# One-word transfers in place of additions as gates of weight reads, two more gates, two sums moved, and another place for one operand

## The chip, the cores and the metric

The kernel runs on one core of a Trainium2 chip. The metric is the device time of one execution in microseconds (us), the median of several runs. TensorE (PE) does the matmuls, VectorE (DVE) and ScalarE (ACT) the elementwise work, GpSimd (POOL) some sums, and SyncE (SP) and POOL issue the transfers, each on a queue of its own. The kernel before takes 1507.99 us (three runs, 1507.09 to 1509.15).

## What is computed

A linear attention, whose output x has 4608 tokens of 512 values, goes through two feed-forward layers. Both have the same form, with weights of their own (512 x 2048 and back); in short:

```python
x = softmax(q, axis=-1) @ (softmax(k, axis=2).T @ v)   # per batch and head
for w_in, w_out in ((moe_w_in, moe_w_out), (moe2_w_in, moe2_w_out)):
    h = np.maximum(x @ w_in, 0.0)
    x = (h * h) @ w_out
```

Everything is float32.

## The kernel before, in words

**Sweeps and blocks.** The four products with weights are four sweeps f = 0 to 3 (`w_in` and `w_out` of the first layer, then of the second), each over 9 blocks j of 512 tokens. A float32 product is made of three matmuls on operands that were split into a high and a low part (`passes`, L444). In sweep 0 the blocks 0 to 5 are plain (`h`). All else is Strassen's scheme: 2 x 2 blocks and seven products instead of eight, so every operand is a tile of seven slices, high and low: two are blocks of the matrix itself (512 of its 1792 columns), five are sums or differences (1280).

**Names.** `n` are the products of sweep 0 from the token operand `v`, `y` those of sweeps 1 and 3 from the hidden operand `G` and the weight operand `W`, `m` those of sweep 2 from `x` and `W`. Names in full are `Wf_a` for operand a (0 to 7) of sweep f, `Gl_j_a` for layer l and block j, `xj_kk`; the page leaves the numbers out. In sweeps 1 and 3 a block takes its 8 operands in turn, seven products on each (`second_mm`, L506), and only at the end are its results made. In sweep 2 (and blocks 6 to 8 of sweep 0) a block has four units u of 84 matmuls (`first_mm`, L457); unit u uses the weight operands 2u and 2u+1. Where one sweep ends and the next begins the work of both is interleaved; the second sweep's first products come before the first one's last ones. These places are called first crossing (sweep 0 to 1), second (1 to 2) and third (2 to 3).

**How an operand is made.** A 512 KB load brings a matrix into SBUF. DVE makes the sums (`comb_add`, L96), ACT the high part (`comb_hi`, L108), DVE the low part (`comb_lo`, L121). A hidden operand is squared by ACT first, in place, in the tile that was loaded (`g_square`, L441; tiles `qc`, `qd`, `qe` by turns). `comb_hi` also sets where an operand lies in its tile: G, x and v have an offset of 8 words (PLAIN), 4 (EARLY) for G0_0_0 and all of x0, and others in layer 1. Of `v` the first high slice alone lies 4 words ahead of its place; `low` holds that view, and `first_mm` takes it for the product that reads this slice.

**Weights.** Weight operands in KEPT (L45) were made once and stored whole. They come as one read of 1792 KB by `get_operand` (L190), on POOL's queue. The others come as 512 KB (`get_w`, L175; tiles `qx`, `qa`) on SP's queue and are combined by DVE and ACT. Operand a goes to slot (a + 5) % 8 of eight, so that a read needs the slot's former operand to be done with. Four reads have a gate as well, by the table `behind` (L804): `touch` (L186), an addition of one word on POOL that reads from a loaded tile, goes ahead of the read in POOL's order. For W2_2 and W2_3 that tile is G0_8_7's.

**Order.** Every step is recorded with an engine, a model cost and a due time. A list scheduler (L604) runs the model and writes out each engine's order: on each engine, of the steps that could start the one with the earliest due time. The engines run their queues in this order and wait on semaphores.

**After the products.** `copy` (L475) takes two products out of PSUM, `both` (L478) adds them on POOL (on DVE for the first Strassen block), `rest` (L481) subtracts, `summed` (L487) and `plus` (L517) make results, `plus2` (L520) on POOL finishes those of sweep 1.

Of the kernel before, what the change touches and what calls it, by code (L numbers as in the profile page):

```python
# [21 lines left out]
P = 128  # L22
# [26 lines left out]
def linear_attention_two_relu2_ffn(ctx: ExitStack, tc: tile.TileContext, q0, k0, eye, qh, kh, vh, wio, out):  # L49
# [58 lines left out]
    def comb_hi(key, q, x, tag):  # L108
        if key not in hls:
            if key[0] in "Gxv":  # L110
                t = pool.tile([P, 14 * HB + SHIFT], F32R, name=key, tag=tag)
                o = LATE + 4 * (key in ("G1_0_0", "G1_0_1", "G1_2_0")) if key[:2] == "G1" else EARLY if key == "G0_0_0" or key[:2] == "x0" else PLAIN
                hls[key] = t[:, o:o + 14 * HB].rearrange("p (a b n) -> p a b n", a=2, b=7)
                if key[0] == "v":
                    low[key] = t[:, o - 4:o - 4 + 2 * (HB + 4)].rearrange("p (a n) -> p a n", a=2)[:, :, :HB]
            else:
                hls[key] = pool.tile([P, 2, 7, HB], F32R, name=key, tag=tag)
        r, src = (slice(0, 2), q[:, 0:4:3]) if x == 0 else (slice(2, 7), cfs[key])
        nc.scalar.activation(out=low[key] if x == 0 and key in low else hls[key][:, 0, r], in_=src, func=AF.Copy)  # L119
# [63 lines left out]
    def put_operand(f, a):  # L183
        nc.sync.dma_start(out=ready_w[f, a], in_=f32(hls.pop(f"S{f}_{a}")))

    def touch(f, a, key):  # L186
        one = pool.tile([P, 1], F32, name=f"touch{f}_{a}", tag="kvm")
        nc.gpsimd.tensor_tensor(out=one, in0=gq[key][:, 0, 0:1], in1=gq[key][:, 0, 0:1], op=ALU.add)  # L188

    def get_operand(f, a, tag):  # L190
        hls[f"W{f}_{a}"] = pool.tile([P, 2, 7, HB], F32R, name=f"W{f}_{a}", tag=tag)
# [265 lines left out]
    def first_mm(l, j, u, i, place):  # L457

        k, o = (l, j, u), BANK[i]
        if i == o:  # L460
            m[k, o] = bank(place, f"{'nm'[l]}{i}_{j}_{u}")
        for s in range(2):
            w = hls[f"W{2 * l}_{2 * u + s}"]
            terms = []
            for kk in range(2):
                x, c = hls[f"{'vx'[l]}{j}_{kk}"], slice(kk * P, (kk + 1) * P)
                high = x[:, 0, RIGHT[i]] if l or RIGHT[i] else low[f"v{j}_{kk}"][:, 0]
                terms.append((w[:, 0, LEFT[i], c], w[:, 1, LEFT[i], c], high, x[:, 1, RIGHT[i]]))
            passes(m[k, o][:, s], terms, start=i == o and s == 0)

# [330 lines left out]
    def slot_of(a):  # L801
        return f"w{(a + 5) % 8}"

    g_loads, g_place, behind = {}, {}, {(2, 2): (0, NB - 1, 7), (2, 3): (0, NB - 1, 7), (3, 5): (1, 0, 4), (3, 7): (1, 0, 6)}  # L804

    def weights(f, a, due):

        if (f, a) in KEPT:
            place = Place(slot_of(a))
            b = behind.get((f, a))  # L810
            if b:
                assert b in g_loads, (f, a)
            seen = op("POOL", 200, due - 9000, lambda: touch(f, a, b), [g_loads[b]], [g_place[b]]) if b else None
            l = op("POOL", 1400, due - 9000, lambda: get_operand(f, a, slot_of(a)), [*kept[f, a], seen, begun.get((f, a))], [place], lands=1792, port=False)
            combined[f"W{f}_{a}"] = [l], place
            return
        beside = Place(slot_of(a + 1)) if f == 0 and a not in (2, 7) else None
        place, new = quad_place("quad", 0, beside) if beside else quad_place(("qx", "qa")[a % 2] if f else "qc")
        after = [dma(due - 12000, lambda: get_w(f, a, new), 512, stashed[f, a], [place])]
        if beside:  # L820
            cf = Place("five", parent=beside), lambda: beside.area(4 * HB, 5 * HB).rearrange("p (a n) -> p a n", n=HB)
        else:
            cf = cf_place(("cf", ("att1", "att2")[a % 2], "att1", "att1")[f])
        combine(f"W{f}_{a}", slot_of(a), due, ("DVE",) * 3, lambda: wfs[f, a], place, after, *cf)
# [175 lines left out]
    def first(l, j, u):  # L1000
# [28 lines left out]
        c2 = copy_of(2, d + g)  # L1029
        mm(5, d + g, [M[2]])  # L1030
        c5 = copy_of(5, d + 2 * g)
        if (l, j) == (0, FIRST):
            s = op("DVE", dve(512), d + 3 * g, lambda: both(k, "DVE"), [c2, c5], [tt["s5"], tt["s2"]], port=True)
        else:
            s = op("POOL", gps(512), d + 3 * g, lambda: both(k), [c2, c5], [tt["s5"], tt["s2"]])
# [20 lines left out]
    def second(l, j, a):  # L1056
# [35 lines left out]
        for q, i, o, po in ((0, 7, 2, p21), (3, 6, 1, p12)):  # L1092
            tt[q] = t_place[k, q] = Place("t")
            if quick:
                y = op("DVE", dve(512), e + 2900, lambda q=q, o=o: plus3(k, q, o), [r, po], [tt[q], tt[o], tt["e"]], port=True)
                y = op("DVE", dve(512), e + 3000, lambda q=q, i=i: plus4(k, q, i), [y, M[i]], [tt[q], bk[i]])
            else:
                y = op("DVE", dve(512), e + 3000, lambda q=q, i=i: summed(k, q, i), [r, M[i]], [tt[q], bk[i], tt["s5"]])
                y = op("POOL", gps(512), e + 3600, lambda q=q, o=o: plus2(k, q, o), [y, po], [tt[q], tt[o]])
            y_stored[k, q] = dma(e + 5000, lambda q=q: put_y(k, q), 256, [y], [tt[q]])  # L1100

    spare = {}
# [139 lines left out]
```

## Time and profile before

| | |
|---|---|
| median of 3 runs | 1507.99 us |
| profiled execution | 1511.11 us |
| its span | 1509.3 us |
| busy PE / DVE / ACT / POOL | 1487.6 / 1190.4 / 971.0 / 253.6 us |
| DMA, mean over the span | 216 GB/s |

The rows come from the profiled execution alone; it lasted 3.1 us longer than the median of the runs, 1.8 us of it lie outside the span. Times of rows are microseconds from the span's start. `W<-o` is a read of a kept weight operand, `qx<-w` a 512 KB load, `[2.05 <-DVE t L488]` says that the engine stood idle for 2.05 us until DVE's `t` of line 488 was there.

### The profile page before, as it was taken

What the parts mean: (1) busy time and instruction counts of PE and PEld (TensorE: products, weight loads), DVE (VectorE), ACT (ScalarE), POOL (GpSimd) and SP (SyncE); (2) the same over time, 40 slices, a digit from 0 to 9 for tenths busy, and PEclk for the clock granted to TensorE, in tenths of its full rate; (3) what the DMA queues carried; (4) which work ended last, traced back from release to release, by engine and by line L of the source; (5) the groups of instructions that cost most, each with busy time, mean ns of one, the idle gap of its engine ahead of it and who ended that gap; (6) DMA issues with size and microseconds to landing.
All of it is one profiled execution on the core that took longest, in us unless ns stands there. A gap on an engine that the chain in (4) does not pass through costs nothing.

```text
span 1509.3 us, 30549 instructions
## 1 busy us (share of the span) xinstructions
PE 1487.6 (99%) x12036; PEld 1414.4 (94%) x12036; DVE 1190.4 (79%) x1823; ACT 971.0 (64%) x1617; POOL 253.6 (17%) x193
## 2 busy tenths in 40 slices
PE   6999999999999999999999999999999999999998
PEld 5788888789999999999999999999999999999998
DVE  7998777899867999999986455444456999999996
ACT  8987767787765666666654788787777443444442
POOL 1001000000110111111113153243311111111110
PEclk9999999999999999999999999999999999999999
DMA  9888989986759444444447677677669644444441
GB/s 368 287 292 319 342 319 336 346 295 204 228 189 328 167 146 138 140 139 140 140 139 273 222 233 257 206 259 249 197 202 325 207 146 136 138 137 138 138 137 55
DMA packets 154144, 326.63 MB, mean 216 GB/s; under 512 B 13072, under 2 KB 84880, under 8 KB 151184
## 3 DMA queue, kind: packets, MB, share of 16 engines
q1 hardware_dynamic: 152128, 300.83, 59.5%
q0 software_dynamic: 1872, 23.86, 4.4%
q8 instruction: 94, 1.54, 0.4%
q14 instruction: 50, 0.41, 0.1%
HBM read 189.63 MB, written 135.00 MB: 215 GB/s over the span
## 4 chain that ended last, share of the span: by engine, by line
PE 90%; DMA 3%; ACT 3%; DVE 2%; issue 1%; POOL 1%; SPq 0%; DVEq 0%; ACTq 0%; POOLq 0%
PE y L448 44%; PE m L448 22%; PE h L448 15%; PE n L448 5%; PE xps L405 2%; PE kvps L334 1%; DMA qx<-w 1%; DMA W<-o 1%; POOL touch L188 0%; ACT w L153 0%; ACT wf L162 0%; DMA w<-w 0%; DMA w<-wio 0%; DMA qc<-w 0%; DMA att<-vh 0%
## 5 line engine op out<-in xcount | busy, mean ns | idle before, releaser
L448 PE MATMUL y<-G,W 128*128 128x256 f32 x3024 | 345.3, 277 | 2.0 <-DVE t L488 2.0
L448 PE MATMUL m<-x,W 128*128 128x256 f32 x3024 | 345.7, 277 | 1.5 <-DMA W<-o 1.5
L448 PEld LDWEIGHTS y<-G,W 128*128 128x128 f32 x3024 | 344.8, 188 | 2.2 <-DVE t L488 2.2
L448 PEld LDWEIGHTS m<-x,W 128*128 128x128 f32 x3024 | 345.1, 188 | 1.7 <-DMA W<-o 1.7
L448 PE MATMUL y<-W,G 128*128 128x256 f32 x3024 | 343.9, 276 | 0.0
L448 PEld LDWEIGHTS y<-W,G 128*128 128x128 f32 x3024 | 343.7, 188 | 0.0
L448 PE MATMUL h<-hl,w 128*128 128x512 f32 x1080 | 259.9, 396 | 3.4 <-DVE w L84 3.4
L448 PEld LDWEIGHTS h<-hl,w 128*128 128x128 f32 x1080 | 200.4, 188 | 49.6 <-DVE w L84 5.7
L479 POOL TENSOR_TENSOR ts<-ts,ts 128x512 f32<-128x512 f32 x61 | 93.5, 1533 | 750.2 <-DVE t L518 460.4
L119 ACT ACTIVATE G<-hl 128x1280 fp32r<-128x1280 f32 (+1 forms) x95 | 86.4, 926 | 115.9 <-PE y L448 65.5
L488 DVE TENSOR_TENSOR t<-m,ts 128x512 f32<-128x512 f32 x72 | 49.1, 688 | 97.5 <-PE m L448 77.9
L125 DVE TENSOR_TENSOR G<-hl,G 128x512 fp32r<-128x512 f32 (+1 forms) x95 | 108.7, 1149 | 16.2 <-ACT G L119 15.2
L448 PE MATMUL n<-v,W 128*128 128x256 f32 x1008 | 120.3, 280 | 0.0
L448 PEld LDWEIGHTS n<-v,W 128*128 128x128 f32 x1008 | 117.1, 188 | 2.1 <-issue 1.7
L491 ACT ACTIVATE t<-t 128x512 f32<-128x512 f32 x96 | 59.8, 628 | 56.2 <-DVE t L488 51.8
L494 ACT ACTIVATE t<-t 128x512 f32<-128x512 f32 x144 | 88.5, 627 | 2.3
L125 DVE TENSOR_TENSOR G<-cf,G 128x1280 fp32r<-128x1280 f32 x51 | 79.7, 1562 | 7.9 <-ACT G L119 7.3
L125 DVE TENSOR_TENSOR G<-att,G 128x1280 fp32r<-128x1280 f32 x49 | 75.9, 1549 | 8.4 <-ACT G L119 7.6
L319 POOL PARTITION_ALL_REDUCE m<-m x28 | 27.0, 964 | 310.5 <-DVE m L315 187.0
L435 ACT ACTIVATE r<-h 128x512 f32<-128x512 f32 x96 | 56.8, 593 | 20.6 <-PE h L448 14.8
L521 POOL TENSOR_TENSOR t<-t,t 128x512 f32<-128x512 f32 x34 | 61.0, 1817 | 42.0 <-DVE t L488 42.0
L119 ACT ACTIVATE G<-cf 128x1280 fp32r<-128x1280 f32 x51 | 64.5, 1265 | 5.6 <-DVE cf L106 5.5
(199 smaller groups left out, 1888.5 us busy)
## 6 DMA issues: line engine op xcount, KB each, us to landing
g<-t SPq DMA_DIRECT2D x192, 256.0 KB, 4.0
hl<-g SPq DMA_DIRECT2D x51, 512.0 KB, 3.8
raw<-wio SPq DMA_DIRECT2D x48, 512.0 KB, 5.3
g<-r SPq DMA_DIRECT2D x96, 256.0 KB, 5.2
W<-o POOLq DMA_DIRECT2D x13, 1792.0 KB, 9.5
y<-t SPq DMA_DIRECT2D x72, 256.0 KB, 2.4
w<-wf SPq DMA_DIRECT2D x64, 256.0 KB, 5.4
o<-S SPq DMA_DIRECT2D x9, 1792.0 KB, 8.3
```

The costliest lines, as they stand in the source:

```text
L119: nc.scalar.activation(out=low[key] if x == 0 and key in low else hls[key][:, 0, r], in_=src, func=AF.Copy)
L125: nc.vector.tensor_tensor(out=hl[:, 1, r], in0=src, in1=f32(hi), op=ALU.subtract)
L319: nc.gpsimd.partition_all_reduce(m[:, 1, :P], m[:, 0, :P], P, bass.bass_isa.ReduceOp.max)
L334: nc.tensor.matmul(ps[j * D:(j + 1) * D, 0:D + 1], k[lo:, c, j * D:(j + 1) * D], v[lo:, c, j, :], start=(c == 0), stop=(c == KC - 1),)
L405: nc.tensor.matmul(ps[:, r], begin[b % 2][p], q[:, r], start=True, stop=True)
L435: nc.scalar.activation(out=r0[j, f].rearrange("p a b -> p (a b)"), in_=m.pop(("h", j, f)), func=AF.Relu)
L448: nc.tensor.matmul(ps, a, b, start=start, stop=True, skip_group_check=True)
L479: (nc.gpsimd if eng == "POOL" else nc.vector).tensor_tensor(out=t[k, "s5"], in0=t[k, "s5"], in1=t[k, "s2"], op=ALU.add)
L488: nc.vector.tensor_tensor(out=temp(k, q), in0=m[k, i], in1=t[k, "s5"], op=ALU.add)
L491: nc.scalar.activation(out=t[k, q], in_=t[k, q], func=AF.Relu)
L494: nc.scalar.activation(out=t[k, q], in_=t[k, q], func=AF.Square)
L521: nc.gpsimd.tensor_tensor(out=t[k, q], in0=t[k, q], in1=t[k, o], op=ALU.add)
```

## The change

- `touch` no longer adds on POOL; it issues a transfer of one word, from the loaded tile to a small array `seen` in HBM, on POOL's queue. For the planner it costs 600 instead of 200 and doesn't share DVE's port.
- W1_5 and W1_7 get gates too: the 512 KB loads of W1_4 and W1_6.
- W2_2's gate becomes the load of G0_8_6 (tile `qd_16`) instead of G0_8_7 (tile `qe_16`). In the planner W2_5 follows the landing of W2_3.
- The sum `both` of block 0, unit 0 of the second layer goes to DVE. The two `plus2` of the last block of sweep 1 are due 6000 ns later.
- x0 lies at PLAIN instead of EARLY, and only its first high slice lies 4 words ahead, as in `v`.

```diff
-                o = LATE + 4 * (key in ("G1_0_0", "G1_0_1", "G1_2_0")) if key[:2] == "G1" else EARLY if key == "G0_0_0" or key[:2] == "x0" else PLAIN
+                o = LATE + 4 * (key in ("G1_0_0", "G1_0_1", "G1_2_0")) if key[:2] == "G1" else EARLY if key == "G0_0_0" else PLAIN
-                if key[0] == "v":
+                if key[0] == "v" or key[:2] == "x0":
                     low[key] = t[:, o - 4:o - 4 + 2 * (HB + 4)].rearrange("p (a n) -> p a n", a=2)[:, :, :HB]
...
+    seen = dram.tile([len(KEPT), 1], F32, name="seen", tag="seen")
     def touch(f, a, key):
-        one = pool.tile([P, 1], F32, name=f"touch{f}_{a}", tag="kvm")
-        nc.gpsimd.tensor_tensor(out=one, in0=gq[key][:, 0, 0:1], in1=gq[key][:, 0, 0:1], op=ALU.add)
+        t = gq[key] if len(key) == 3 else wfs[key]
+        x = KEPT.index((f, a))
+        nc.gpsimd.dma_start(out=seen[x:x + 1], in_=t[0:1, 0, 0:1])
...
-                high = x[:, 0, RIGHT[i]] if l or RIGHT[i] else low[f"v{j}_{kk}"][:, 0]
+                high = x[:, 0, RIGHT[i]] if RIGHT[i] or (l and j) else low[f"{'vx'[l]}{j}_{kk}"][:, 0]
...
-    g_loads, g_place, behind = {}, {}, {(2, 2): (0, NB - 1, 7), (2, 3): (0, NB - 1, 7), (3, 5): (1, 0, 4), (3, 7): (1, 0, 6)}
+    g_loads, g_place, behind = {}, {}, {(1, 5): (1, 4), (1, 7): (1, 6), (2, 2): (0, NB - 1, 6), (2, 3): (0, NB - 1, 7), (3, 5): (1, 0, 4), (3, 7): (1, 0, 6)}
...
-            seen = op("POOL", 200, due - 9000, lambda: touch(f, a, b), [g_loads[b]], [g_place[b]]) if b else None
-            l = op("POOL", 1400, due - 9000, lambda: get_operand(f, a, slot_of(a)), [*kept[f, a], seen, begun.get((f, a))], [place], lands=1792, port=False)
+            gate = op("POOL", 600, due - 9000, lambda: touch(f, a, b), [g_loads[b]], [g_place[b]], lands=1, port=False) if b else None
+            l = op("POOL", 1400, due - 9000, lambda: get_operand(f, a, slot_of(a)), [*kept[f, a], gate, *(combined["W2_3"][0] if (f, a) == (2, 5) else ()), begun.get((f, a))], [place], lands=1792, port=False)
...
-        if (l, j) == (0, FIRST):
+        if (l, j) == (0, FIRST) or k == (1, 0, 0):
             s = op("DVE", dve(512), d + 3 * g, lambda: both(k, "DVE"), [c2, c5], [tt["s5"], tt["s2"]], port=True)
...
-                y = op("POOL", gps(512), e + 3600, lambda q=q, o=o: plus2(k, q, o), [y, po], [tt[q], tt[o]])
+                y = op("POOL", gps(512), e + 3600 + 6000 * (k == (0, NB - 1)), lambda q=q, o=o: plus2(k, q, o), [y, po], [tt[q], tt[o]])
```

**Where instructions move.** POOL's order at the first crossing, before. `W_3`, `W_5` and `W_7` are the reads of W1_3, W1_5 and W1_7, `ts_0_8_2` and `ts_0_8_3` the sums `both` of the last two units of sweep 0.

```order
50 L479 TENSOR_TENSOR ts_0_8_2_5361<-ts_0_8_2_5361,ts_0_8_2_5344 128x512
51 L192 DMA W_3_5394<-o_3_114 128x3584
52 L479 TENSOR_TENSOR ts_0_8_3_5488<-ts_0_8_3_5488,ts_0_8_3_5472 128x512
53 L192 DMA W_5_5520<-o_5_115 128x3584
54 L192 DMA W_7_5650<-o_7_116 128x3584
55 L479 TENSOR_TENSOR ts_0_0_6030<-ts_0_0_6030,ts_0_0_6009 128x512
```

The reads of W1_5 and W1_7 follow the last sum with nothing between.

After (the changed kernel's line numbers are 3 or 4 higher: L191 is `touch`, L195 `get_operand`, L482 `both`):

```order
50 L482 TENSOR_TENSOR ts_0_8_2_5362<-ts_0_8_2_5362,ts_0_8_2_5345 128x512
51 L195 DMA W_3_5395<-o_3_114 128x3584
52 L482 TENSOR_TENSOR ts_0_8_3_5489<-ts_0_8_3_5489,ts_0_8_3_5473 128x512
53 L191 DMA seen<-qx_5456 1x1
54 L195 DMA W_5_5608<-o_5_115 128x3584
55 L191 DMA seen<-qx_5610 1x1
56 L195 DMA W_7_5831<-o_7_116 128x3584
57 L482 TENSOR_TENSOR ts_0_0_6036<-ts_0_0_6036,ts_0_0_6027 128x512
```

Each of the reads of W1_5 and W1_7 now has a one-word transfer ahead of it, from the tile `qx` into which the 512 KB of W1_4 and W1_6 are loaded. POOL waits there for that load.

POOL's order at the second crossing, before. `touch_2` and `touch_3` are the additions, `qe_9448` is the tile of G0_8_7, `ts_0_8` the sum `both` of block 8 of sweep 1, `ts_1_0_0` that of the first unit of sweep 2, and `t_0_8` the two `plus2`.

```order
79 L192 DMA W_0_9347<-o_0_117 128x3584
80 L192 DMA W_1_9368<-o_1_119 128x3584
81 L188 TENSOR_TENSOR touch_2_9579<-qe_9448 128x1
82 L188 TENSOR_TENSOR touch_3_9582<-qe_9448 128x1
83 L192 DMA W_2_9593<-o_2_118 128x3584
84 L192 DMA W_3_9611<-o_3_120 128x3584
85 L192 DMA W_5_9629<-o_5_121 128x3584
86 L479 TENSOR_TENSOR ts_0_8_9682<-ts_0_8_9682,ts_0_8_9674 128x512
87 L479 TENSOR_TENSOR ts_1_0_0_9742<-ts_1_0_0_9742,ts_1_0_0_9660 128x512
88 L521 TENSOR_TENSOR t_0_8_9744<-t_0_8_9744,t_0_8_9696 128x512
89 L521 TENSOR_TENSOR t_0_8_9747<-t_0_8_9747,t_0_8_9704 128x512
90 L479 TENSOR_TENSOR ts_1_0_1_9856<-ts_1_0_1_9856,ts_1_0_1_9812 128x512
```

Both additions stand ahead of all three reads, and the reads ahead of the sums.

After (`qd_9363` is the tile of G0_8_6; L524 is `plus2`):

```order
81 L195 DMA W_0_9350<-o_0_117 128x3584
82 L195 DMA W_1_9371<-o_1_119 128x3584
83 L191 DMA seen<-qd_9363 1x1
84 L195 DMA W_2_9576<-o_2_118 128x3584
85 L191 DMA seen<-qe_9451 1x1
86 L195 DMA W_3_9681<-o_3_120 128x3584
87 L482 TENSOR_TENSOR ts_0_8_9679<-ts_0_8_9679,ts_0_8_9671 128x512
88 L524 TENSOR_TENSOR t_0_8_9761<-t_0_8_9761,t_0_8_9695 128x512
89 L524 TENSOR_TENSOR t_0_8_9763<-t_0_8_9763,t_0_8_9703 128x512
90 L195 DMA W_5_9802<-o_5_121 128x3584
91 L482 TENSOR_TENSOR ts_1_0_1_9852<-ts_1_0_1_9852,ts_1_0_1_9837 128x512
```

W2_2 and W2_3 each have a gate of their own in front, on different tiles; W2_5 has gone behind `both` and the two `plus2` of block 8; the sum `ts_1_0_0` has left POOL. On ACT no instruction moves, but the square of `qd_16` (G0_8_6) waits for one semaphore more than before, that of the transfer `seen<-qd_9363`, which reads the tile that the square overwrites.

## Rows read from the trace of the kernel before

**Rows 1.** The page: busy time of the engines, and the last chain by line.
```profile
PE 1487.6 (99%) x12036; PEld 1414.4 (94%) x12036; DVE 1190.4 (79%) x1823; ACT 971.0 (64%) x1617; POOL 253.6 (17%) x193
PE y L448 44%; PE m L448 22%; PE h L448 15%; PE n L448 5%; PE xps L405 2%; PE kvps L334 1%; DMA qx<-w 1%; DMA W<-o 1%; POOL touch L188 0%; ACT w L153 0%; ACT wf L162 0%; DMA w<-w 0%; DMA w<-wio 0%; DMA qc<-w 0%; DMA att<-vh 0%
```

**Rows 2.** PE's waits: engine, line, released by, us in total, times, longest.
```profile
PE y L448 <- DVE t L488: 2.0, 1, 2.0
PE m L448 <- DMA W<-o: 1.5, 1, 1.5
```

**Rows 3.** Windows: stretch, us, busy by engine (count), granted clock, DMA share, GB/s.
```profile
460.00:470.00 10.00, 10.00 (x90) 10.00 (x88) 2.71 (x5) 3.93 (x6) 1.17 (x2) 1.00 1.06 410
474.00:479.00 5.00, 4.58 (x26) 4.58 (x27) 3.91 (x6) 4.60 (x7) 0.00 (x0) 0.66 0.92 274
822.00:825.00 3.00, 1.55 (x13) 1.34 (x13) 1.70 (x2) 1.26 (x3) 0.81 (x1) 1.00 1.05 418
```

**Rows 4.** Timeline, first crossing: start, duration, instruction, [idle time before it, what ended it].
```profile
456.16 0.70 SPq L177 DMA_DIRECT2D qx<-w  x1
...
461.57 0.57 POOL L192 DMA_DIRECT2D W<-o  x1 [0.96 <-PE n L448]
...
469.30 0.69 DVE L102 TENSOR_TENSOR att<-qx 128x512 f32<-128x512 f32 x1 [5.95 <-DMA qx<-w]
...
473.68 1.28 DVE L488 TENSOR_TENSOR t<-n,ts 128x512 f32<-128x512 f32 x2
...
474.42 0.85 PE L448 MATMUL y<-G,W 128*128 128x256 f32 x3 [2.05 <-DVE t L488]
```

**Rows 5.** Weight read issued from 461 to 462, us to its landing.
```profile
DMA to landing us min/median/max: 9.9/9.9/9.9
```

**Rows 6.** Timeline, second crossing, the engines of the prediction.
```profile
795.74 14.44 PE L448 MATMUL y<-G,W 128*128 128x256 f32 x126
...
797.70 1.04 ACT L442 ACTIVATE qd<-qd 128x1024 f32<-128x1024 f32 x1
...
799.24 0.68 DVE L102 TENSOR_TENSOR cf<-qd 128x512 f32<-128x512 f32 x1
...
802.78 1.48 DVE L125 TENSOR_TENSOR G<-cf,G 128x1280 fp32r<-128x1280 f32 x1
...
804.11 7.57 POOL L188 TENSOR_TENSOR touch<-qe 128x1 f32<-128x1 f32 x2 [16.90 <-ACT qe L442]
...
809.87 1.48 DVE L125 TENSOR_TENSOR G<-att,G 128x1280 fp32r<-128x1280 f32 x1
...
811.45 4.93 PE L448 MATMUL y<-G,W 128*128 128x256 f32 x42
...
811.71 1.64 POOL L192 DMA_DIRECT2D W<-o  x3
...
819.83 2.98 POOL L521 TENSOR_TENSOR t<-t,t 128x512 f32<-128x512 f32 x2
...
819.90 0.69 DVE L482 TENSOR_TENSOR ts<-m,ts 128x512 f32<-128x512 f32 x1 [0.51 <-POOL ts L479]
...
824.27 0.98 PE L448 MATMUL m<-x,W 128*128 128x256 f32 x6 [1.45 <-DMA W<-o]
```

**Rows 7.** Weight reads issued from 786 to 790, and from 811 to 813.
```profile
L192 POOL DMA_DIRECT2D W<-o x1: 527/527/527, 786.7 to 786.7; - x1
DMA to landing us min/median/max: 13.9/13.9/13.9
...
DMA to landing us min/median/max: 7.6/12.0/16.7
```

**Rows 8.** Windows of 26 us, TensorE alone: `v`, then x0, then x1.
```profile
420.00:446.00 26.00, 26.00 (x230) 1.00 0.58 193
826.00:852.00 26.00, 26.00 (x220) 1.00 0.84 293
866.00:892.00 26.00, 26.00 (x232) 1.00 0.74 233
```

More of the change, by code (lines that the diff above doesn't have):

```diff
@@ L810, in weights @@
             b = behind.get((f, a))
-            if b:
-                assert b in g_loads, (f, a)
-            seen = op("POOL", 200, due - 9000, lambda: touch(f, a, b), [g_loads[b]], [g_place[b]]) if b else None
-            l = op("POOL", 1400, due - 9000, lambda: get_operand(f, a, slot_of(a)), [*kept[f, a], seen, begun.get((f, a))], [place], lands=1792, port=False)
+            gate = op("POOL", 600, due - 9000, lambda: touch(f, a, b), [g_loads[b]], [g_place[b]], lands=1, port=False) if b else None
+            l = op("POOL", 1400, due - 9000, lambda: get_operand(f, a, slot_of(a)), [*kept[f, a], gate, *(combined["W2_3"][0] if (f, a) == (2, 5) else ()), begun.get((f, a))], [place], lands=1792, port=False)
             combined[f"W{f}_{a}"] = [l], place
@@ L819, in weights @@
         after = [dma(due - 12000, lambda: get_w(f, a, new), 512, stashed[f, a], [place])]
+        g_loads[f, a], g_place[f, a] = after[0], place
         if beside:
```

## The prediction

> **What bounds the kernel now.** I read the page's busy times and its chain first. TensorE is busy for 1487.6 us of a span of 1509.3 us, and the chain that ended last is four fifths `y`, `m` and `h` matmuls [rows 1]. So time can come from two things only: a matmul that gets cheaper, or a stretch in which TensorE stands still. The waits of PE name the stretches: after the start of the program there are two that this change can reach, 2.0 us for a DVE result in `y` and 1.5 us for a weight read in `m` [rows 2]. Then I read the granted clock around both. After the first, at the first crossing, the five microseconds 474 to 479 have a mean granted clock of 0.66; around the second it is 1.00 [rows 3]. So the first stall costs 2.05 us and then (1 - 0.66) x 5 = 1.7 us more, since TensorE runs at the lower of its levels for a while; the second costs its 1.45 us alone. Last I read the two crossings instruction by instruction.
>
> **The gates of W1_5 and W1_7.** What held `y` at 474.42 was DVE's `t` sum at 473.68. That sum stood in DVE's queue behind the combination of W1_4, whose first operation had sat idle for 5.95 us until the 512 KB load of `qx` landed at 469.30. The load had been issued at 456.16, 13.1 us earlier. At 461.57 POOL had issued the 1792 KB read of W1_5 beside it [rows 4], and that read was under way for 9.9 us [rows 5]. The transfers shared one limit: from 460 to 470 the core moved 410 GB/s with its DMA engines full [rows 3]. The change holds the W1_5 read until just this `qx` load has landed. Its 1.84 MB are 4.5 us of the bus at 410 GB/s, so the load can land between 469.30 - 4.5 = 464.8 and, if the bus is owed to others, where it lands now. With an even share from about 462.6 on, half of the 6.7 us to 469.3 went to W1_5, and the load lands near 466.0; I take that. From the landing to the restart of TensorE it was 474.42 - 469.30 = 5.1 us. TensorE ran out of work at 474.42 - 2.05 = 472.37. So a landing before 467.25 removes the stall whole, and mine has 1.2 us to spare. **Term: -2.05 - 1.7 = -3.75 us**, with the ends -4.0 (the hole before it closes too) and 0 (the load is late for another reason). Behind the new wait on POOL stand only the two reads. `y` spends 42 matmuls, 4.8 us, on an operand [rows 6]; the restart is at the last product of operand 0, so W1_5 and W1_7 are wanted some 20 and 30 us later. Read some 4.5 us later than now, they are still there in time: that costs nothing, and with the slack gone each would cost what it lands late, up to 4.5 us.
>
> **The place of x0.** In a stretch of 26 us at full clock the trace holds 220 matmuls while `m` reads x0, and 230 in a stretch of sweep 0 that reads `v` operands [rows 8]. x0 lies 4 words early as a whole; `v` has only its first high slice there, which is what x0 gets now. So a matmul on x0 takes 26/220 = 118.2 ns and one on `v` 26/230 = 113.0. Block 0 of `m` has 4 units of 84 matmuls. **Term: 336 x 5.1 ns = -1.7 us.** Bounds: 0, if the place isn't the cause, and -2.05 at the pace of the stretch with 232. The transfers are no rival cause: they move 193 GB/s in the one stretch and 293 in the other, but the stretch 866 to 892 (x232, 233 GB/s) stands at the fast pace with nearly as much. x0 is written by operations of the same sizes on the same engines; PE has no wait for it now, and that costs nothing.
>
> **The second crossing: what goes.** At 804.11 POOL ran two `touch` additions of one word each, which took 7.57 us together: DVE worked without a gap meanwhile. Only then, at 811.71, did POOL issue the three reads of W2_2, W2_3 and W2_5 [rows 6]. They landed 7.6, 12.0 and 16.7 us after their issue [rows 7], one after the other, and `m` waited 1.45 us for the middle one until 824.27 [rows 6]. Now the gates are transfers, which DVE can't stretch: W2_2 goes when `qd` has landed, before ACT's square of it at 797.70; W2_3 when `qe` has been squared, at 804.1 now and about 807 with the shift below. Even with 12 us to land, W2_3 is there at 819, before its first use at 824.27 - 1.45 = 822.8. **Term: -1.5 us**, with a bound of 0 if W2_3 is still late.
>
> **The second crossing: what comes.** The word that opens W2_2 is read from the tile `qd_16`, and ACT squares that tile in place. The order shows ACT's square (at 797.70 now) with one more wait, for the completion of that very transfer: it may not overwrite what is still being read. The transfer stands on POOL's queue behind the read of W2_1, issued at 786.7 and landed 13.9 us later, at 800.6 [rows 7]. No row shows a one-word transfer. From below: it completes as soon as it is issued, the square starts when it does now, cost 0. From above: it completes only with the read of W2_2 issued behind it, which is the worst that a queue in order can do, and that is the rival on the other side below (some +9). The three reads that landed one after the other are the nearest row: this queue finished them in order. So I let the word complete with W2_1, and the square start near 801.0, 3.3 us late.
> The Trainium skill has a rule on this (DMA: Bandwidth & Descriptors, Why a DMA increments its semaphore by 16 and not by 1): on the software path all 16 engines post their increment, whatever the transfer's shape, each after its own data. So even one word waits for every engine's share of the read ahead of it. The spaced landings agree with it, and it speaks against this change; by it the next sum holds, without it the next sum would be 0.
> DVE's first sum from that tile is at 799.24 now; behind a square that ends at 801.0 + 1.04 it comes 2.8 us late. DVE is full from there (in the touch's 7.57 us it left no gap): its low part of G0_8_6 (802.78 + 1.48 = 804.3 now) ends at 807.1, and that of G0_8_7 (809.87 + 1.48 = 811.35 now) at 814.2 [rows 6]. `y` runs 126 matmuls in 14.44 us up to 810.18, 42 on each operand, so G0_8_6 begins at 805.3, and after 12 matmuls that need only its first two slices the rest is wanted at 806.6: 0.6 us short. Then `y` on G0_8_7 begins at 811.45 + 0.6, wants the rest 1.4 us later, at 813.4, and gets it at 814.3: 0.9 us short. **Term: +1.5 us**, ends 0 and +10.
>
> **The rest, at nothing.** W2_5 goes behind two `plus2`, which end at 819.83 + 2.98 = 822.8 [rows 6]; 1.5 us later by the shift above, and with 7.6 to 11 us to land it is there at 832 to 835.4. Its first use is 84 matmuls behind 824.27, about 834: 0, at most +1.2 us. The sum `both` of (1,0,0) moves to DVE, where it takes the room of an idle 0.51 us that waited for POOL's version [rows 6]. A gate in front of a read in sweep 3 replaces two `touch`, and `y` waits for no weights there.
>
> **Sum** against the profiled execution of 1511.11 us (1509.3 of span and 1.8 around it): -3.75 - 1.7 - 1.5 + 1.5 = -5.4 us, so 1505.7. The median of the runs shown is 3.1 us lower, at 1507.99; from it the forecast is **1502.6 us**.
>
> **Rivals.**
> *The word holds nothing.* If the one-word transfer overtakes or finishes early, the +1.5 is gone: -6.9, 1501.1 us. For it: one word against 1.84 MB. Against it: the landings in order.
> *The first stall stays.* If the `qx` load is late for another reason (the stores `g<-t` on its own queue), or if an unprofiled run never has that stall, only -1.7 is left: 1506.3 us. For it: the load was already 5.4 us old when W1_5 was issued, and hadn't landed. Between the two, the stall shrinks to under a microsecond and the clock stays up: 1503 to 1504.
> *The place isn't what slows x0.* Then -3.7: 1504.3 us. Against it: x1, read by the same code, runs at x232.
> *The other side: the word completes only behind the read of W2_2.* That read lands 4.4 to 7.6 us after W2_1's, the steps of rows 7, at 805.0 to 808.2. The square is then 7.7 to 10.9 us late and DVE 7.2 to 10.4, `y` on G0_8_6 stands until 811.6 to 814.8 where it wanted the rest at 806.6, 0.9 us more go on G0_8_7, and after a hole longer than 2.05 us the clock falls as after 474, +1.7 us: 7.6 to 10.8 us. Against the gains of 6.95 that is about +2 us: 1510.3. It comes out slower from a completion after some 804.5 on. For it: nothing in the trace; against it: a transfer has no claim on a later one.
>
> **How the numbers follow.** The forecast has a chance of 0.50, the word that holds nothing 0.20, the first stall that stays 0.17, the place of x0 0.07, the other side 0.06. The range reaches from a little under the word that holds nothing, 1500.5, to the stall that stays, 1506.5 us. A difference under 0.2% (3.0 us) can't be told from none. Faster by more than that are the forecast, the word that holds nothing and the place of x0, 0.50 + 0.20 + 0.07: 0.77, since the part of the stall that stays below 1505 about makes up for the forecast's above it. Within 0.2% lie the rest of that case and a little of the other side, 0.18; slower is most of the other side, 0.05.
>
> **What would show it.** Right: PE's waits without the 2.0 us for DVE and without the 1.5 us for `W<-o`; granted clock 1.00 from 474 to 479; the `qx` load landing by 467; about 230 matmuls in 26 us on x0; ACT's square of `qd` near 801, and two new waits of PE on G before 815. Wrong: the same landing of `qx` at 469; a square at 798; a wait of `m` for W2_5 near 834; or any new stretch at 0.50 clock.

## The result and the profile after

The changed kernel takes 1517.39 us (median of 17 runs, 1510.78 to 1525.98), the kernel before 1508.3 (17 runs beside them): the ratio over all these runs is 1.0064, 95% interval [1.0045, 1.0084]. The forecast was 1502.6 us, a gain; the kernel became slower instead. The times of both kernels fall into two groups, so each kernel is given below by the median of its lower group and by the number of its runs more than 9 us above its fastest:

| kernel | lower group | the others |
|---|---|---|
| changed, 17 runs | 9, 1510.8 to 1517.4, median 1513.6 | 8, 1521.0 to 1526.0, median 1522.9 |
| before, 133 runs over all comparisons | 121, 1506.2 to 1512.0, median 1508.0 | 12, 1516.0 to 1523.5 |

The profiled execution took 1525.73 us, so it belongs to the upper group. The page of the changed kernel, its span and its busy times, answers to [rows 1]:

```profile
span 1523.9 us, 30561 instructions
...
PE 1501.1 (98%) x12036; PEld 1427.5 (94%) x12036; DVE 1189.5 (78%) x1824; ACT 972.0 (64%) x1617; POOL 250.0 (16%) x194
```

TensorE is busy 13.5 us longer than before with the same 12036 matmuls, so most of the 14.6 us aren't stops. Its waits (engine, line, released by; total, times, longest), where [rows 2] had two others:

```profile
PE m L451 <- ACT t L488: 2.2, 1, 2.2
PE y L451 <- DVE G L125: 1.6, 1, 1.6
PE y L451 <- ACT G L119: 0.8, 1, 0.8
PE y L451 <- DVE t L491: 0.3, 1, 0.3
PE y L451 <- DVE ts L485: 0.3, 1, 0.3
```

Both old stops are gone. The windows of the changed kernel (columns as in [rows 3] and [rows 8], TensorE alone):

```profile
474.00:479.00 5.00, 5.00 (x47) 1.00 0.96 333
802.00:809.00 7.00, 4.64 (x26) 0.76 0.35 104
816.00:842.00 26.00, 26.00 (x230) 1.00 0.76 267
843.00:852.00 9.00, 6.95 (x46) 0.81 0.54 176
866.00:892.00 26.00, 26.00 (x224) 1.00 0.66 210
```

At 474 the granted clock is 1.00, where [rows 3] had 0.66. The stretch on x0 has 230 matmuls, as forecast. But the clock falls at two new places, behind 803 (0.76) and behind 843 (0.81), and behind the second one 26 us hold 224 matmuls where [rows 8] had 232, at a granted clock of 1.00. That pace lasts: from 860 to 1160 there are 2550 matmuls against 2649 before, 117.6 ns each instead of 113.3. This time from one matmul to the next is called the pace below; a short window also counts the matmuls that its ends cut, so that a quotient from it comes out 1 to 2 ns lower. The timeline of the changed kernel at the first crossing, then at the second:

```profile
465.98 0.69 DVE L102 TENSOR_TENSOR att<-qx 128x512 f32<-128x512 f32 x1 [2.38 <-DMA qx<-w]
...
472.46 2.82 PE L451 MATMUL y<-G,W 128*128 128x256 f32 x23
...
796.34 0.52 POOL L191 DMA_DIRECT2D seen<-qd  x1 [11.64 <-DMA qd<-g]
...
800.86 1.06 ACT L445 ACTIVATE qd<-qd 128x1024 f32<-128x1024 f32 x1 [5.58 <-DMA seen<-qd]
...
803.66 0.38 PE L451 MATMUL y<-G,W 128*128 128x256 f32 x1 [0.75 <-ACT G L119]
...
805.65 6.36 PE L451 MATMUL y<-G,W 128*128 128x256 f32 x41 [1.61 <-DVE G L125]
...
824.67 0.59 POOL L195 DMA_DIRECT2D W<-o  x1
...
828.24 1.23 SPq L548 DMA_DIRECT2D xq<-y  x2
...
841.50 0.72 DVE L102 TENSOR_TENSOR cf<-xq 128x512 f32<-128x512 f32 x1 [6.08 <-DMA xq<-y]
...
845.05 17.19 PE L451 MATMUL m<-x,W 128*128 128x256 f32 x131 [2.16 <-ACT t L488]
```

The landings of the read of W2_1 and of five of the one-word transfers in the changed kernel, from their issue (the last two have one answer: 7.4 for `seen<-qd`, 3.8 for `seen<-hl`):

```profile
L195 POOL DMA_DIRECT2D W<-o x1: 530/530/530, 784.2 to 784.2; - x1
DMA to landing us min/median/max: 15.0/15.0/15.0
...
L191 POOL DMA_DIRECT2D seen<-qx x1: 518/518/518, 478.2 to 478.2; - x1
DMA to landing us min/median/max: 5.0/5.0/5.0
...
L191 POOL DMA_DIRECT2D seen<-qd x1: 518/518/518, 796.3 to 796.3; - x1
DMA to landing us min/median/max: 4.5/4.5/4.5
...
L191 POOL DMA_DIRECT2D seen<-qe x1: 518/518/518, 806.7 to 806.7; - x1
DMA to landing us min/median/max: 1.6/1.6/1.6
...
L191 POOL DMA_DIRECT2D seen<-qd x1: 518/518/518, 1151.5 to 1151.5; - x1
...
L191 POOL DMA_DIRECT2D seen<-hl x1: 518/518/518, 1185.2 to 1185.2; - x1
...
DMA to landing us min/median/max: 3.8/5.6/7.4
```

The `qx` load lands at 465.98 (466.0 was forecast) and TensorE goes through 472. ACT's square waits for the one-word transfer, which lands 4.5 us after its issue, at 800.8; the read of W2_1 ahead of it (issued at 784.2, 15.0 us) had landed at 799.2. TensorE then stops twice. Later x1's loads, issued at 828.24 instead of 825.29, land after 13 us beside the read of W2_5; ACT's queue waits for them ahead of a ReLU that is to free the memory into which TensorE writes next, and TensorE stops for 2.16 us.

More moved than POOL's order: the traces show DVE's and ACT's instructions in another order than before between about 482 and 580 and between 805 and 850, and one store more on SP's queue ahead of x1's loads. The pauses near 510 and at 843 lie in these stretches; that no instruction moves on ACT, as said of the change, isn't so.

A rough sum of this one execution, in us: first crossing -3.75; x0, 228 matmuls up to the stop at 843, -1.2; W2_3 -1.45; small stops near 510 +0.6; the two at 803 and 805 +2.36 and the clock (1 - 0.76) x 7 = +1.7; the one at 843 +2.16 and (1 - 0.81) x 9 = +1.7; the slow pace from 850 to 1186, 2854 matmuls x 4.4 ns, +12.6. Together +14.7; the two profiled executions differ by 14.6.

### The profile page after: what moved, and what is told of

Read it like the earlier page. It is cut to its first block, busy times and chain, and to the rows that moved or that the text cites. A ratio compares the mean times of both kernels' runs of the same rounds, so it can differ in the third digit from the quotient of the medians.

```text
span 1523.9 us, 30561 instructions
## 1 busy us (share of the span) xinstructions
PE 1501.1 (98%) x12036; PEld 1427.5 (94%) x12036; DVE 1189.5 (78%) x1824; ACT 972.0 (64%) x1617; POOL 250.0 (16%) x194
## 4 chain that ended last, share of the span: by engine, by line
PE 88%; DMA 5%; issue 3%; ACT 2%; DVE 1%; POOL 0%; SPq 0%; DVEq 0%; ACTq 0%; POOLq 0%
PE y L451 41%; PE m L451 22%; PE h L451 16%; PE n L451 6%; PE xps L408 2%; PE kvps L337 2%; DMA qx<-w 1%; DMA w<-wio 1%; DMA xq<-y 1%; DMA att<-vh 0%; DMA w<-wf 0%; DMA w<-vh 0%; DMA w<-q 0%; DMA seen<-qd 0%; ACT wf L162 0%
## 5 line engine op out<-in xcount | busy, mean ns | idle before, releaser
L451 PE MATMUL m<-x,W 128*128 128x256 f32 x3024 | 357.8, 281 | 2.2 <-ACT t L488 2.2
L451 PEld LDWEIGHTS m<-x,W 128*128 128x128 f32 x3024 | 357.2, 190 | 2.4 <-ACT t L488 2.4
L482 POOL TENSOR_TENSOR ts<-ts,ts 128x512 f32<-128x512 f32 x60 | 90.9, 1514 | 759.7 <-DVE t L521 430.6
L119 ACT ACTIVATE G<-hl 128x512 fp32r<-128x512 f32 (+1 forms) x95 | 86.3, 926 | 116.9 <-PE y L451 66.4
L524 POOL TENSOR_TENSOR t<-t,t 128x512 f32<-128x512 f32 x34 | 63.5, 1888 | 41.4 <-DVE t L491 41.4
```

What stands on the lines that cost most here:

```text
L451: nc.tensor.matmul(ps, a, b, start=start, stop=True, skip_group_check=True)
L482: (nc.gpsimd if eng == "POOL" else nc.vector).tensor_tensor(out=t[k, "s5"], in0=t[k, "s5"], in1=t[k, "s2"], op=ALU.add)
L524: nc.gpsimd.tensor_tensor(out=t[k, q], in0=t[k, q], in1=t[k, o], op=ALU.add)
```

## The experiments

Four theories came up in turn. A: the stop near 843 makes the later matmuls slow. B: x0's new place does. C: it is chance. D: each stop draws the pace anew. "Old order" means that no other instruction moves.

**1. One gate back.** `gate_back`:

```diff
-    g_loads, g_place, behind = {}, {}, {(1, 5): (1, 4), (1, 7): (1, 6), (2, 2): (0, NB - 1, 6), (2, 3): (0, NB - 1, 7), (3, 5): (1, 0, 4), (3, 7): (1, 0, 6)}
+    g_loads, g_place, behind = {}, {}, {(1, 5): (1, 4), (1, 7): (1, 6), (2, 2): (0, NB - 1, 7), (2, 3): (0, NB - 1, 7), (3, 5): (1, 0, 4), (3, 7): (1, 0, 6)}
```

> The changed kernel with one entry of the table `behind` undone: W2_2 is gated by G0_8_7 again, so ACT's square of qd_16 no longer waits for a one-word transfer. In the planner's order the loads of x1 also go ahead of the stores g<-t again. Theory A (TensorE's stop near 843 us, from the late x1, is what makes the later `m` matmuls slow, 117.7 instead of 113 ns): no stop, no slow pace, the whole gain of about 7 us stays, 1501 us. Theory B (x0's new place makes the later `m` matmuls slow): the pace is still 117.7 ns, about 1513 us. Theory C (executions fall into the slow pace by chance, whatever stands before): a mixture of both.

Lower group 1517.8 (5 runs), the other six from 1527.3 to 1542.5. The planner moved much else, and new stops came: on W2's reads 2.1 us, on ACT's `ts` 2.6. None of the theories' numbers came out. But in its profile sweep 2 runs at 113 ns, and sweep 1 at 117.4 (852 matmuls from 600 to 700).

**2. x1's loads earlier.** `xq_early`:

```diff
-        ld = dma(d - 20000, lambda: load_y(j, kk, tag), 512, [y_stored[(0, j), q] for q in range(4)], [place], held=8000 if j in (1, 2) else None)
+        ld = dma(d - 20000 - 6000 * (j == 1), lambda: load_y(j, kk, tag), 512, [y_stored[(0, j), q] for q in range(4)], [place], held=8000 if j in (1, 2) else None)
```

> The changed kernel with the two loads of x1 due 6 us earlier in the planner, so that they go ahead of the stores; the gates stay as they are, and with them ACT's wait for the one-word transfer and the stops near 803 us. Theory A: no stop near 843, `m` at 113 ns; the gains of 7 us less about 4 us for the stops near 803 and the clock behind them, 1505 us. Theory B: still 117.7 ns after x0, 1516 us. Theory C: a mixture.

Lower group 1512.7 (8), 4 above 1521. Here too sweep 1 is the slow one, from a stop of 1.3 us at 511 on. A and B both speak of sweep 2 alone, so neither explains it.

**3. x0's place alone.** `x0_only`, the kernel before with the edits of `comb_hi` and `first_mm`; old order.

> The kernel before with x0's new place alone; no instruction moves. Theory A: x0's 336 matmuls at 113 instead of 118.2 ns, the rest as before: -1.7 us, 1506.6 us. Theory B: the later `m` matmuls at 117.7 ns, +12 us, 1518 us. Theory C: mostly 1506.6, some at 1518.

Lower group 1507.6 (8 runs, 0.3 below that of the kernel before), 4 above 1517. Its profile has no sweep at the slow pace, against B. It shows something else: the stop at 472 isn't there. TensorE at the first crossing in this run, with the same order there as before:

```profile
471.68 1.53 PE L448 MATMUL n<-v,W 128*128 128x256 f32 x12
473.05 3.16 PE L448 MATMUL y<-G,W 128*128 128x256 f32 x26
```

The other traced executions with the old order here stop at this place for times of their own: `seen_only`, `hole` and `square_wait` (experiments 6, 4 and 9) as follows, `holes` (experiment 5) not at all. So the stop comes and goes from one execution to the next.

```profile
PE y L451 <- DVE t L491: 2.2, 1, 2.2
...
PE y L448 <- DVE t L490: 1.4, 1, 1.4
...
PE y L452 <- DVE t L492: 0.7, 1, 0.7
```

The slow pace does show for a moment in `x0_only`: behind the stop on W2_3 there are 87 matmuls from 821.5 to 831.5, then 90 from 833 to 843, still on x0 and with no pause between.

**4. A stop put in.** `hole`, the kernel before with one ReLU nine times:

```diff
+        for _ in range(9 if (k, q) == ((1, 0, 2), 2) else 1):
             nc.scalar.activation(out=out, in_=m[k, i], func=AF.Relu)
```

> The kernel before, with one ReLU of ACT in unit 2 of block 0 of sweep 2 done nine times instead of once (5 us of ACT), so that TensorE stops for some microseconds near 843 us for want of a free bank. Theory A: a stop of 2 to 5 us, 1.7 us for the clock, and then the `m` matmuls at 117.7 ns until 1180: 1520 to 1527 us. Theories B and C: the stop and the clock alone, 1512 to 1515 us, and `m` at 113 ns from block 1 on.

Lower group 1513.3 (8), 4 above 1522. In the profile the stops are 3.8 us and the granted clock from 851 to 860 is 0.81 on average, but `m` then runs at 113 ns (354 matmuls from 860 to 900): A doesn't hold as a rule.

**5. Fourteen stops.** `holes`, the kernel before with such repeats in blocks 1 to 7 of sweeps 1 and 2:

```diff
+        for _ in range(9 if k[0] and 0 < k[1] < 8 and len(k) == 3 and k[2] == 2 and q == 2 else 1):
             nc.scalar.activation(out=out, in_=m[k, i], func=AF.Relu)
...
+        for _ in range(2 + 2 * k[1] if len(k) == 2 and k[0] == 0 and 0 < k[1] < 8 and i == 2 else 1):
             nc.scalar.activation(out=out, in_=m[k, i], func=AF.Copy)
```

> The kernel before with one ACT copy or ReLU repeated (4 to 16 times) near the start of each of blocks 1 to 7 in sweeps 1 and 2, to stop TensorE there 14 times; it computes the same. Theory D: the pace of the matmuls changes at these stops and nowhere else, some blocks at 113 and some at 117.7 ns. Rival (the pace is set once, where a sweep begins): every block of a sweep runs at one pace, whatever stops stand between.

One run, 1559.43 us. Three blocks in a row of sweep 2, each behind a stop (timeline of `holes`, TensorE), and then windows inside them:

```profile
955.97 39.84 PE L448 MATMUL m<-x,W 128*128 128x256 f32 x336 [1.66 <-ACT t L489]
997.35 38.36 PE L448 MATMUL m<-x,W 128*128 128x256 f32 x336 [1.55 <-ACT t L489]
1038.10 41.24 PE L448 MATMUL m<-x,W 128*128 128x256 f32 x336 [2.38 <-ACT t L489]
```

```profile
965.00:995.00 30.00, 30.00 (x257) 1.00 0.80 261
1000.00:1035.00 35.00, 35.00 (x312) 1.00 0.75 253
1050.00:1075.00 25.00, 25.00 (x215) 1.00 0.63 203
```

30.0/257 = 116.7 ns, then 35.0/312 = 112.2, then 25.0/215 = 116.3: the pace changes at the stops and holds between them, at a granted clock of 1.00. Most other blocks run at the faster pace; in sweep 1 eight stops of 1.1 to 6.4 us all leave it as it is. So the rival doesn't hold. D does here, but not without exception: `x0_only` changed its pace near 832 without a stop.

**6. Transfers for additions.** `seen_only`, the kernel before with the new `touch`; old order.

> The kernel before with its four `touch` additions replaced by one-word transfers on POOL's queue, in the same places: every other instruction of every engine stands where it stood. Theory D (every longer stop of TensorE draws anew whether the matmuls behind it run at 113 or at 117.7 ns, until the next stop or a change of the operand's place; a sweep at 117.7 costs about 11 us): POOL issues the reads at about 804.5 instead of 811.7, the stop of 1.45 us at 822.8 goes, nothing else stops: 1506.8 us, and slow executions no more often than before. Rival (a one-word transfer itself disturbs, by a wait or by POOL's queue): 1508 or more, or a new wait in PE's list.

1506.69, ratio 0.9998 [0.9974, 1.0021] (lower group 1506.5, 2 above 1519): the wait for W2_3 is gone from the trace. The median moved by -1.3, near the term of -1.5, though all runs taken together can't be told from those of the kernel before.

**7. The two first gates alone.** `w1_gates`, put in where the read is issued; old order:

```diff
+        if (f, a) in ((1, 5), (1, 7)):
+            nc.gpsimd.dma_start(out=seen[a // 7:a // 7 + 1], in_=wfs[f, a - 1][0:1, 0, 0:1])
         nc.gpsimd.dma_start(out=hls[f"W{f}_{a}"], in_=ready_w[f, a])
```

> The kernel before with one-word transfers ahead of the reads of W1_5 and W1_7 and nothing else; every other instruction stands where it stood. Theory D: the stop of 2.05 us at 472 and the clock's fall behind it go, 3.75 us there. DVE's work for block 0's end at 507 to 513 then comes up short by what the stop had given it: a stop of 0 to 2 us near 510, so 1504.2 to 1506.5 us in fast executions, and if that stop is there some executions 11 us longer with sweep 1 at 117.7 ns. Rival (the gate of the stop is given back in full at 510): 1508 us.

1507.86, ratio 1.0001 [0.9981, 1.0021] (lower group 1507.8, 2 above 1517). No stop at 472, none near 510, and no gain: the rival's number, by another way than it said.

**8. x0's old place in the changed kernel.** `place_undone`; no move.

> The changed kernel with x0 back at its old place (all of it 4 words early); no instruction moves against the changed kernel. Theory D with the addition that the change of place between x0 and x1 sets the pace anew and at 113 ns: sweep 2 no longer runs at 117.7 ns behind the stop near 843; slow executions come from sweep 1 alone and are rarer than 8 in 17; x0 costs 1.7 us more. Fast executions at 1513 to 1516 us. Rival (x0's place does nothing to the pace behind it): as many slow executions as the changed kernel has, at 1522 to 1527 us.

1515.2 to 1526.4 in 7 runs, six of them above 1519: undoing the place doesn't heal it. In the profile sweep 1 is at 117.4 ns from a stop near 510 on, sweep 2 at 113. Whether the change of place sets the pace can't be told from seven runs.

**9. The wait of the square, added.** `square_wait`, the kernel before with one transfer; old order:

```diff
+        if (j, a) == (NB - 1, 6):
+            nc.gpsimd.dma_start(out=seen, in_=gq[0, j, a][0:1, 0, 0:1])
         nc.scalar.activation(out=gq[0, j, a], in_=gq[0, j, a], func=AF.Square)
```

> The kernel before with one transfer more: a word of qd_16 on POOL's queue behind the read of W2_1, ahead of ACT's square of that tile in the program; nothing else moves. If the word completes only behind W2_1's read: the square starts near 801 instead of 797.7, TensorE stops twice on G (near 806 and 813) for 1 to 2.5 us together, 1509 to 1510.5 us. If the word isn't held: the square at 798, no new stop, 1508 us.

1509.97, ratio 1.0022 [0.9998, 1.0045], 2.0 us above the runs beside it; lower group 1509.9, 2 above 1521. The word is held (timeline of `square_wait`):

```profile
798.16 0.56 POOL L445 DMA_DIRECT2D seen<-qd  x1 [10.10 <-DMA qd<-g]
803.15 1.06 ACT L446 ACTIVATE qd<-qd 128x1024 f32<-128x1024 f32 x1 [4.51 <-DMA seen<-qd]
807.93 4.97 PE L452 MATMUL y<-G,W 128*128 128x256 f32 x41 [1.55 <-DVE G L125]
```

**10. The wait, removed.** `wait_undone`, the changed kernel with the word read behind the square; no other move:

```diff
-        nc.gpsimd.dma_start(out=seen[x:x + 1], in_=t[0:1, 0, 0:1])
+        if (f, a) != (2, 2):
+            nc.gpsimd.dma_start(out=seen[x:x + 1], in_=t[0:1, 0, 0:1])
...
         nc.scalar.activation(out=gq[0, j, a], in_=gq[0, j, a], func=AF.Square)
+        if (j, a) == (NB - 1, 6):
+            nc.gpsimd.dma_start(out=seen[3:4], in_=gq[0, j, a][0:1, 0, 0:1])
```

> The changed kernel with the word of qd_16 read behind ACT's square instead of ahead of it, so that the square no longer waits for it; no other instruction moves. If the wait was the main cost of the change: no stops near 803 and 805, no fall of the clock there, fast executions at 1509 to 1510 us instead of 1513, fewer slow ones. Rival (TensorE only meets the next late operand sooner): the stop near 843, on ACT behind x1's late loads, grows by what the stops near 803 gave, and fast executions stay at 1512 to 1514 us.

1510.7, ratio 1.0030 [1.0000, 1.0060]; lower group 1509.2 (8), 4 above 1520. The wait cost 4.4 us of the lower group, the largest single part of it. What is left in the traced execution, one of the long ones, are two stops, on sums and on ACT (waits of `wait_undone`):

```profile
PE m L454 <- ACT t L491: 1.8, 1, 1.8
PE y L454 <- DVE ts L488: 1.2, 1, 1.2
```

**11 and 12. The good parts in the old order.** `best_a` is `seen_only` with the two gates of `w1_gates`; `best_b` has x0's new place too.

> The kernel before with one-word transfers in place of the `touch` additions and with the gates of W1_5 and W1_7, every instruction in the old order. Both stops of TensorE in sweeps 1 and 2 should go. Theory D: 1505 to 1506.5 us, slow executions (11 us more) no oftener than 1 in 12, since no stop is left that draws the pace anew. Rival (the pace is drawn where a sweep begins): as many slow ones as the kernel before has or more.

> As best_a, with x0's new place as well. Without a stop in sweep 2: 1.2 to 1.7 us less than best_a, 1503.5 to 1505 us, slow executions as rare. Rival (x0's old place sets the pace right where x1 begins, and the new one doesn't): a third of the executions 11 us longer, as in the kernel with x0's new place alone.

`best_a` 1505.76 (lower group 1505.5, 3 of 11 above 1517); `best_b` 1504.29, all eleven from 1503.28 to 1505.87, ratio 0.9971 [0.9955, 0.9988]: it beats both kernels. The place of x0 is worth 1.2 us between the two. Neither profile has a stop longer than 0.32 us in the sweeps 1 to 3, so why three runs of `best_a` are long is open: no trace shows one of them.

**13. The gates by the planner.** `planned_w1`, `best_b` with W1's gates in the table `behind`; DVE's, ACT's and PE's order moves near 485 to 515 as in the changed kernel:

```diff
-        if (f, a) in ((1, 5), (1, 7)):
-            x = KEPT.index((f, a))
-            nc.gpsimd.dma_start(out=seen[x:x + 1], in_=wfs[f, a - 1][0:1, 0, 0:1])
...
-    g_loads, g_place, behind = {}, {}, {(2, 2): (0, NB - 1, 7), (2, 3): (0, NB - 1, 7), (3, 5): (1, 0, 4), (3, 7): (1, 0, 6)}
+    g_loads, g_place, behind = {}, {}, {(1, 5): (1, 4), (1, 7): (1, 6), (2, 2): (0, NB - 1, 7), (2, 3): (0, NB - 1, 7), (3, 5): (1, 0, 4), (3, 7): (1, 0, 6)}
```

> best_b with the gates of W1_5 and W1_7 put in through the planner, as in the changed kernel: the same transfers on POOL, but 43 rows of DVE's and ACT's order and some of PE's between about 485 and 515 stand as in the changed kernel. If this order makes the stop near 510: a stop on DVE's ts there, 0.5 to 2 us, fast executions at 1505 to 1506.5 us, and about a third of all at 1514 to 1518 us with sweep 1 at 117.7 ns. Rival (the stop near 510 is no more than TensorE being earlier, whatever the order): best_b again, 1504.3 us, since it is as early.

1506.55; lower group 1506.0 (10 runs, spread 1503.4 to 1509.9), 2 above 1515. The profiled run took 1505.64 and has no stop near 510. Whether the new order costs anything is open: the lower group lies 1.7 above that of `best_b`, but spreads over 6.5 us.

**14. The regrouped sums.** `regroup`, `best_b` with the other planner edits:

```diff
-            l = op("POOL", 1400, due - 9000, lambda: get_operand(f, a, slot_of(a)), [*kept[f, a], seen, begun.get((f, a))], [place], lands=1792, port=False)
+            l = op("POOL", 1400, due - 9000, lambda: get_operand(f, a, slot_of(a)), [*kept[f, a], seen, *(combined["W2_3"][0] if (f, a) == (2, 5) else ()), begun.get((f, a))], [place], lands=1792, port=False)
...
-        if (l, j) == (0, FIRST):
+        if (l, j) == (0, FIRST) or k == (1, 0, 0):
...
-                y = op("POOL", gps(512), e + 3600, lambda q=q, o=o: plus2(k, q, o), [y, po], [tt[q], tt[o]])
+                y = op("POOL", gps(512), e + 3600 + 6000 * (k == (0, NB - 1)), lambda q=q, o=o: plus2(k, q, o), [y, po], [tt[q], tt[o]])
```

> best_b with what the change does to the planner at the second crossing: W2_5 behind W2_3, `both` of (1,0,0) on DVE, the two `plus2` 6 us later; W2_2's gate stays on G0_8_7, so nothing waits for a one-word transfer. If the later W2_5 and the moved sums make the stop near 843: a stop there of 1 to 4 us, fast executions at 1506 to 1508 us, some 11 us longer. Rival (the stop near 843 came from the stores that went ahead of x1's loads, which isn't so here): 1504.3 us.

1505.57; lower group 1504.9 (8), 4 above 1516. The stop on ACT is 0.9 us, and the lower group hardly differs from `best_b`. The profiled run is a long one, 1517.36, and can be laid beside that of `best_b`. At one place in sweep 1, where block 2 begins (both orders are the same there), both waited shortly for DVE. Windows of `best_b`, TensorE; the timeline's row of its wait; and the windows of `regroup`:

```profile
526.00:546.00 20.00, 20.00 (x179) 1.00 0.37 127
552.00:572.00 20.00, 20.00 (x179) 1.00 0.39 136
600.00:700.00 100.00, 100.00 (x885) 1.00 0.43 138
```

```profile
549.15 51.09 PE L454 MATMUL y<-G,W 128*128 128x256 f32 x448 [0.32 <-DVE ts L488]
```

```profile
526.00:546.00 20.00, 20.00 (x178) 1.00 0.38 126
540.00:560.00 20.00, 19.96 (x173) 1.00 0.52 165
552.00:572.00 20.00, 20.00 (x172) 1.00 0.38 135
600.00:700.00 100.00, 100.00 (x852) 1.00 0.40 129
```

Before it both have the fast pace (179 and 178 in 20 us). Behind a wait of 0.32 us `best_b` keeps it (885 in 100 us); behind one of 0.04 us (19.96 busy of 20) `regroup` has 852, and keeps that until sweep 2. So the slow pace can begin at a pause of a fraction of a microsecond. It costs some 270 us x (1 - 852/885) = 10 us here.

## Why the prediction was wrong

- **The first gain wasn't in the median.** The step at 472 went as worked out, landing, stop and clock alike, and none of the ten traced executions with the two new gates stops there. But -3.75 was taken from one profiled execution and applied to the median, which was 3.1 us lower already. In the old order the stop lasted from 0 to 2.2 us (experiment 3), and the granted clock from 474 to 479 was below 1.00 in the two longest alone (0.66 behind 2.05 us, 0.75 behind 2.2). The executions with the stop stood 3 to 4 us above their kernels' lower groups, `x0_only` without it 0.8 below its own, and of the 121 runs in the lower group of the kernel before only 6 are above 1510. `w1_gates`, which removes the stop, leaves the median as it was (1507.86 against 1507.94); `best_a` lies 1.0 below `seen_only` in the lower group. So the gates are worth 0 to 1 us of the median, not 3.75. The nearest rival, that an unprofiled run never has that stall, was given 0.17. The difference of 3.1 us, which the prediction names, was the sign.
- **The wait of the square was mis-sized.** The wait came, and the square began at 800.86 (801.0 forecast). That the times agree is partly luck: W2_1 landed at 799.2 instead of 800.6, and the word not with it but 1.6 us later. By the Trainium skill (DMA: Bandwidth & Descriptors, Why a DMA increments its semaphore by 16 and not by 1) every engine has to post its increment, and each does so after its own data. The traces agree in the order of landings: sixteen words, in eleven traces, were issued with a weight read of their queue on its way, and each landed 0.2 to 2.0 us behind that read; the one of 1151.5, which took 7.4 us, landed 0.3 us behind it. The 4.5 us of `seen<-qd` alone don't show it, since `seen<-qx` took 5.0 with no read ahead of it but with the DMA engines full (share 0.98), and `seen<-qe` 1.6 with them idle (0.01). The price was +1.5. By itself the wait is a net +2.0, with the stop of 1.45 us on W2_3 gone as well (`square_wait`; the two additions took 1.20 us there instead of 7.57); in the changed kernel it is 2.36 us of stops and 1.7 of clock, 4.4 us of the lower group (`wait_undone`). The step that failed: needs were taken from the old trace, but TensorE wanted G0_8_6 at 802.9 instead of 805.3, by what the first crossing had given, while the word landed no earlier than forecast; and the sum held nothing for the clock.
- **"The rest, at nothing" was wrong.** W2_5 was in time; the transfers beside it weren't. Its later read shares the bus with x1's loads, which the prediction never priced. The first of them is issued 2.95 us later than before, behind one store `g<-t` more and behind a `plus2` that ends 1.9 us later, and lands after 13.2 us where it took 9.7: 2.16 us of stop and 1.7 of clock. That the longer way comes from the read fits `xq_early`, where the two loads go 0.9 us ahead of it and land after 4.9 and 6.8 us, and `regroup`, where they follow it without the store more and take 13.4 and 14.0. How much of the stop is the stores' and how much the bus's isn't told apart: `regroup` stops for 0.9 us, `xq_early` for 1.6 on ACT's `ts` at 852, which waits for a store.
- **The pace wasn't among the rivals.** In six traced executions (the changed kernel, `gate_back`, `xq_early`, `place_undone`, `wait_undone`, `regroup`) one sweep runs at 117 to 118 ns instead of 113, at 10 to 13 us; it begins at a pause of TensorE. In four of them that is a stop of 0.7 to 1.7 us on DVE's `ts` near 511, in the changed kernel's order, where its own traced execution waits for 0.25 and 0.32 us and keeps the fast pace. In the nine others (without `holes`), all of their kernels' lower groups, no whole sweep is slow. The changed kernel has pauses near 510, 803, 805 and 843 and 8 of 17 long runs; the one before 12 of 133. That the other long runs, which have no trace, are of this kind is inferred from their distance of 9 to 12 us.
- **Right:** W2_3's wait (-1.5 forecast, -1.3 in the median of `seen_only`) and x0's place (-1.7 forecast; -1.2 between `best_a` and `best_b`, -0.3 in `x0_only`; 230 matmuls in 26 us). All signs of being right came, and of those of being wrong only the last, new stretches at a lower clock: the crossings went by the mechanisms told, and the time was lost in their sizes and behind them.

What makes a pause draw the slow pace or the fast one stays open, and so does whether a change of an operand's place draws as well, and why `x0_only` changed without a pause.

## What to carry to other kernels

Take a term from a profiled execution only if the median contains it: when the profiled run stands 3 us above the median, look for a stop of that size first. A transfer that reads a tile holds the tile's next writer until it lands, and behind a big read on its queue that is late; so read the word behind the in-place operation (-4.4 us here). And try the parts of an edit one by one in the old order before a list scheduler orders everything again: the transfers, the gates of W1 and x0's place make 1504.3 there (`best_b`), while the whole change without the wait makes 1509.2 in the better runs (`wait_undone`). Which of its other edits costs the 4.9 us isn't shown: at the first crossing alone the new order makes 1506.0 (`planned_w1`), the edits at the second alone 1504.9 (`regroup`).

## What was not expected of the hardware

The interval of one and the same matmul stream (128x128 weights, 256 columns) has two values at a granted clock of 1.00, 112 to 113 and 116 to 118 ns, and goes from one to the other at pauses down to 0.04 us (`regroup`) and where a sweep ends; within a sweep it otherwise held, for 25 us and up to 340, but for one change without a pause (`x0_only`, near 832). A one-word transfer on POOL's queue took 1.6 us with the DMA engines idle and 5.0 with them full, and behind a 1792 KB read on its way it landed 0.2 to 2.0 us after that read.
